# Reordering the first loads of a gated attention/MLP kernel: x tiles 0 and 1 from one ring, the other ring held back, a key matmul between the transposes

## The chip, the cores and the metric

The kernel runs on one core of one Trainium2 chip. The metric is the device time of one execution in microseconds (us). A trace's own span is about 1.7 us shorter than the time reported for that execution. All moments inside a trace are counted from the start of its span. The engines are PE (TensorE, the matmuls), ACT (ScalarE), DVE (VectorE), POOL (GpSimd) and SP (SyncE, which here only issues DMAs). A load "lands" when the trace reports it as complete. "The clock" is that of PE; its record in the trace says when it was full.

## The reference

```python
def reference(A_x, A_wqkv, A_wo, B_x, B_w1, B_b1, B_w2, B_b2, gate_w):
    x = A_x                                              # [1, 2048, 512] bf16
    g = sigmoid((x * gate_w).sum(-1, keepdims=True))
    a = linear_attention(x, A_wqkv, A_wo)                # 32 heads of 16; phi(k) = elu-like + 1e-6
    b = token_mlp(layernorm(x), B_w1, B_b1, B_w2, B_b2)  # 2048 -> 1792 -> 2048 along the tokens
    return g * a + (1 - g) * b
```

Only the first step matters here. The key matmuls read x transposed (`kacc<-wk_sb,xT` in the profile), so the kernel transposes the first four x tiles of 128 rows on TensorE and gets the other twelve from transposing DMAs.

## The kernel before

SP and ACT each issue plain DMAs on their own ring. The first eight loads of 128 KB are x tiles 0 to 3 and the four 128-row chunks of Wk. Behind them SP issues the DMA transposes and everything else. In the listing, `load_x(q, t0, n)` loads x tiles, `load_wk(q, k)` chunk k of Wk, `load_xT(t0, n)` is a DMA transpose from SP.

```python
load_x(nc.sync, 0, 1)
load_x(nc.scalar, 1, 1)
load_wk(nc.sync, 0)
load_x(nc.scalar, 2, 1)
load_x(nc.sync, 3, 1)
for k, q in ((1, nc.scalar), (2, nc.sync), (3, nc.scalar)):
    load_wk(q, k)
load_xT(4, 2)
load_xT(6, 2)
load_x(nc.sync, 4, 4)
# ... [cut: the remaining x tiles, Wq, w1, Wv, Wo, all from SP]
nc.vector.memset(ones_f[:], 1.0)
nc.vector.memset(mhalf[:], -0.5)
nc.vector.memset(Z32[:], 0.0)
# ... [cut: identity and masks on GpSimd]
warm_up(6)                      # six matmuls of 512 columns on a constant, result unused
# ... [cut: definitions]
HEADS = 4
transpose_tile(0, False)        # 4 PE transposes into one tile (pt), then a copy on DVE
transpose_tile(1, True)         # the same, copy on ACT
transpose_tile(2, False)
ln_step(0)
for k in range(2):
    for t in range(HEADS - 1):
        k_part(t, (k,))         # key matmul: tile t, chunk k of Wk, accumulating in kacc
transpose_tile(HEADS - 1, True)
ln_step(1)
for t in range(HEADS):
    k_part(t, range(2 if t < HEADS - 1 else 0, ND))
    k_phi(t)
for t in range(HEADS, NT):      # steady state
    k_part(t, range(ND))
    k_phi(t)
    g_tile(t - LAG)             # gacc: first one at t = 4
    # ... [cut]
```

In the profile `wps` is written by the warm-up matmuls, `pt` by the transposes, `kacc` by the key matmuls, and `gacc` by the matmuls that sum x times phi(k) over the tokens. Before the first gacc matmul PE thus has to do 16 transposes of 128 columns and 20 key matmuls of 512 columns: 6 in the first group (tiles 0 to 2 with Wk chunks 0 and 1) and 14 after tile 3's transposes (tiles 0 to 2 with chunks 2 and 3, tiles 3 and 4 with all four).

Of the kernel before, what the change touches and what calls it, by code (L numbers as in the profile page):

```python
# [15 lines left out]
def kernel(  # L16
# [13 lines left out]
    nc = tc.nc  # L30
# [36 lines left out]
    def keep(shape, dtype, name):  # L67
        return persist.tile(shape, dtype, name=name, tag=name)

    def bank(name, dtype=FP32):  # L70
        return ps.tile([P, SC], dtype, name=name, tag="bank")
# [5 lines left out]
    wk_sb = keep([P, ND, D], BF16, "wk_sb")  # L77
# [7 lines left out]
    Z32 = keep([P, ND * 40], BF16, "Z32")  # L85
# [22 lines left out]
    mhalf = keep([P, TPC], FP32, "mhalf")  # L108
    ones_f = keep([P, 1], FP32, "ones_f")
    warm = nc.const_aps.tensor(1.0, (P, SC), BF16)  # L110

    def mm(o, lhsT, rhs, start, stop, **kw):
        nc.tensor.matmul(o, lhsT=lhsT, rhs=rhs, start=start, stop=stop, **kw)  # L113
# [14 lines left out]
    def load_x(q, t0, n):  # L128
        q.dma_start(out=xs[:, t0 : t0 + n, :], in_=x_view[:, t0 : t0 + n, :])

    def load_wk(q, k):
        q.dma_start(out=wk_sb[:, k, :], in_=wqkv_view[:, k, D : 2 * D])

    def load_xT(t0, n):
        nc.sync.dma_start(
            out=xT[:, :, t0 * P : (t0 + n) * P], in_=X[t0 * P : (t0 + n) * P, :], transpose=True
        )

    load_x(nc.sync, 0, 1)
    load_x(nc.scalar, 1, 1)  # L140
    load_wk(nc.sync, 0)
    load_x(nc.scalar, 2, 1)
    load_x(nc.sync, 3, 1)
    for k, q in ((1, nc.scalar), (2, nc.sync), (3, nc.scalar)):
# [18 lines left out]
            nc.sync.dma_start(out=wv_sb[:], in_=wqkv_view[:, :, 2 * D : 3 * D])  # L163
            nc.sync.dma_start(out=wo_sb[:], in_=wo_view)

    nc.vector.memset(ones_f[:], 1.0)
    nc.vector.memset(mhalf[:], -0.5)
    nc.vector.memset(Z32[:], 0.0)
    nc.gpsimd.memset(ident[:], 0.0)
    nc.gpsimd.affine_select(  # L170
        out=ident[:], in_=ident[:], compare_op=ALU.not_equal, fill=1.0, base=0,
# [18 lines left out]
    def warm_up(n, cols=SC):  # L190
        for _ in range(n):
            mm(wps[:, :cols], warm[:, 0:P], warm[:, :cols], True, True)

    act_warm = keep([P, 1], FP32, "act_warm")
    nc.scalar.activation(out=act_warm[:], in_=ones_f[:], func=ACT.Exp)
    warm_up(6)

    def transpose_tile(t, on_act):
        pt = bank("pt", BF16)
        for k in range(ND):  # L200
            nc.tensor.transpose(pt[:, k * P : (k + 1) * P], xs[:, t, k * P : (k + 1) * P], ident[:])  # L201
        dst = xT[:, :, t * P : (t + 1) * P]
        src = pt[:].rearrange("p (k s) -> p k s", k=ND)
        if on_act:
            nc.scalar.activation(out=dst, in_=src, func=ACT.Copy)
        else:
            nc.vector.tensor_copy(out=dst, in_=src)
# [13 lines left out]
    def k_part(t, ks):  # L221
        if t not in kaccs:
            kaccs[t] = bank("kacc")
        for k in ks:
            mm(
                kaccs[t][:], xT[:, k, t * P : (t + 1) * P], wk_sb[:, k, :],
                k == 0, k == ND - 1,
            )
# [49 lines left out]
    def ln_step(u):  # L278
        ln_stats(u)
        if u % TPC == TPC - 1:  # L280
            ln_rstd(u // TPC)

    HEADS = 4
    transpose_tile(0, False)
    transpose_tile(1, True)
    transpose_tile(2, False)
    ln_step(0)
    for k in range(2):
        for t in range(HEADS - 1):
            k_part(t, (k,))  # L290
    transpose_tile(HEADS - 1, True)
    ln_step(1)
    for t in range(HEADS):
# [243 lines left out]
```

## Time and profile before

| | before |
|---|---|
| time, 4 runs | median 164.31 us (163.93 to 164.63) |
| span of the trace | 162.6 us |
| PE busy | 158.0 us, 97% |
| first transpose | 3.74 us |
| full clock of PE from | 5.73 us |
| first gacc matmul | 9.91 us |

From the profile's page of the kernel before, the busy time of each engine and the chain of waits by engine and line:

```profile
PE 158.0 (97%) x823; PEld 72.9 (45%) x837; DVE 89.5 (55%) x210; ACT 63.3 (39%) x97; POOL 17.5 (11%) x34
...
PE 96%; DMA 2%; issue 1%; DVE 0%
```

PE is the bound; beside short stretches of issuing, the only other thing on the chain of any size is one DMA. The timeline of PE alone in the kernel before, 0 to 9.5 us, merged by group (start, time, engine, line, operation, out<-in, form, count, idle before):

```profile
0.84 2.72 PE L113 MATMUL wps<-const-bfloat16-1.0 128*128 128x512 bf16 x6 [0.84 <-PEq L521]
3.74 1.46 PE L201 MATMUL pt<-ident,xs 128*128 128x128 bf16 x12 [0.17 <-DMA xs<-in_A_x_dram]
4.99 1.84 PE L113 MATMUL kacc<-wk_sb,xT 128*128 128x512 bf16 x6
6.66 0.39 PE L201 MATMUL pt<-ident,xs 128*128 128x128 bf16 x4
6.89 2.97 PE L113 MATMUL kacc<-wk_sb,xT 128*128 128x512 bf16 x13
```

From 3.74 us on PE has nearly always something to do (its longest gap before 9.9 us is 0.04 us). Its speed is not constant. The records of single instructions have transposes 0.107 us apart and 512-column matmuls 0.427 us apart until 5.7 us, and then 0.056 and 0.216 us. Full clock is thus about twice the early one, which is called half clock below. The clock record agrees: full from 5.73 us.

The issues of the two DMA rings in the kernel before up to 3.6 us, SP's and then ACT's, from the timelines of these two engines ("SPq" and "ACTq" are their sequencers; the time is that of issuing, not of moving):

```profile
0.81 0.40 SPq L129 DMA_DIRECT2D xs<-in_A_x_dram  x1
1.27 0.42 SPq L132 DMA_DIRECT2D wk_sb<-in_A_wqkv_dram  x1
1.74 0.43 SPq L129 DMA_DIRECT2D xs<-in_A_x_dram  x1
2.21 0.44 SPq L132 DMA_DIRECT2D wk_sb<-in_A_wqkv_dram  x1
3.52 2.96 SPq L135 DMA_TRANSPOSE xT<-in_A_x_dram  x2
```

```profile
0.80 0.87 ACTq L129 DMA_DIRECT2D xs<-in_A_x_dram  x2
1.70 0.94 ACTq L132 DMA_DIRECT2D wk_sb<-in_A_wqkv_dram  x2
```

### The profile page before, as it was taken

What the parts mean: (1) busy time and instruction counts of PE and PEld (TensorE: products, weight loads), DVE (VectorE), ACT (ScalarE), POOL (GpSimd) and SP (SyncE); (2) the same over time, 40 slices, a digit from 0 to 9 for tenths busy, and PEclk for the clock granted to TensorE, in tenths of its full rate; (3) what the DMA queues carried; (4) which work ended last, traced back from release to release, by engine and by line L of the source; (5) the groups of instructions that cost most, each with busy time, mean ns of one, the idle gap of its engine ahead of it and who ended that gap; (6) DMA issues with size and microseconds to landing.
All of it is one profiled execution on the core that took longest, in us unless ns stands there. A gap on an engine that the chain in (4) does not pass through costs nothing.

```text
span 162.6 us, 2183 instructions
## 1 busy us (share of the span) xinstructions
PE 158.0 (97%) x823; PEld 72.9 (45%) x837; DVE 89.5 (55%) x210; ACT 63.3 (39%) x97; POOL 17.5 (11%) x34
## 2 busy tenths in 40 slices
PE   7999999999999999999999999999999999999992
PEld 2544444444444444444444444444444444444452
DVE  0599999967999999519995401166211111111112
ACT  3463386648667483212865113111122222111110
POOL 3000711200110000001415500050000000000000
PEclk9999999999999999999999999999999999999999
DMA  4999999999900006600892699732000001110001
GB/s 141 252 247 246 278 312 355 382 386 386 281 5 0 0 0 223 228 4 0 272 324 77 209 328 323 279 106 94 32 32 32 32 32 43 48 42 33 32 32 32
DMA packets 30057, 25.05 MB, mean 154 GB/s; under 512 B 7968, under 2 KB 29472, under 8 KB 30048
## 3 DMA queue, kind: packets, MB, share of 16 engines
q1 hardware_dynamic: 28032, 22.02, 42.9%
q0 software_dynamic: 1440, 2.38, 5.5%
q10 hardware_dynamic: 576, 0.52, 1.1%
q8 instruction: 6, 0.10, 0.2%
q14 instruction: 3, 0.02, 0.1%
HBM read 21.11 MB, written 2.23 MB: 144 GB/s over the span
## 4 chain that ended last, share of the span: by engine, by line
PE 96%; DMA 2%; issue 1%; DVE 0%
PE uacc L113 30%; PE yps L113 30%; PE kacc L113 9%; PE aps L113 8%; PE gacc L113 8%; PE qacc L113 8%; DMA xs<-in_A_x_dram 2%; PE pt L201 1%; PE denps L113 1%; PE kvps L113 0%; PE w2ps L113 0%; DVE ot L500 0%; PE pt L330 0%
## 5 line engine op out<-in xcount | busy, mean ns | idle before, releaser
L113 PE MATMUL uacc<-hs,w1c 128*128 128x512 bf16 x219 | 51.0, 379 | 0.4
L113 PE MATMUL yps<-uT,w2c 128*128 128x512 bf16 (+2 forms) x234 | 50.6, 366 | 0.2
L500 DVE SCALAR_TENSOR_TENSOR ot<-yps,c,a_sc 128x512 bf16<-128x512 f32 (+2 forms) x17 | 12.2, 719 | 44.8 <-PE yps L113 41.5
L113 PEld LDWEIGHTS <-w2c 128*128 128x128 bf16 x238 | 22.8, 98 | 25.9
L113 PEld LDWEIGHTS <-w1c 128*128 128x128 bf16 x224 | 21.8, 98 | 26.3 <-issue 0.2
L487 ACT ACTIVATE a_sc<-aps,c,gg 128x512 f32<-128x512 f32 x16 | 12.4, 777 | 46.7 <-PE aps L113 43.0
L324 ACT ACTIVATE uT<-uacc,bcol 128x512 bf16<-128x512 f32 x14 | 9.3, 688 | 21.7 <-PE uacc L113 21.7
L113 PE MATMUL aps<-W2sb,pqT 128*128 128x512 bf16 x63 | 16.2, 379 | 0.1
L113 PE MATMUL qacc<-xT,wq_sb 128*128 128x512 bf16 x63 | 16.2, 379 | 0.0
L113 PE MATMUL kacc<-wk_sb,xT 128*128 128x512 bf16 x63 | 16.1, 385 | 0.0
L113 PE MATMUL gacc<-pk,xs 128*128 128x512 bf16 x62 | 15.5, 379 | 0.1
L251 ACT ACTIVATE hs<-xs,nmr,rstd 128x512 bf16<-128x512 bf16 x16 | 12.8, 805 | 1.9 <-DVE nmr L245 1.9
L211 ACT ACTIVATE e<-qacc 128x512 bf16<-128x512 f32 x16 | 9.6, 597 | 9.2 <-PE qacc L113 8.3
L211 ACT ACTIVATE e<-kacc 128x512 bf16<-128x512 f32 x16 | 9.3, 595 | 6.9 <-PE kacc L113 5.6
L439 POOL DMA_DIRECT2D rex<-rd_dram x16 | 9.4, 598 | 22.9 <-DVE pqT L441 20.1
L215 DVE SCALAR_TENSOR_TENSOR pqT<-qacc,e 128x512 bf16<-128x512 f32 x16 | 11.1, 692 | 0.6
L215 DVE SCALAR_TENSOR_TENSOR pk<-kacc,e 128x512 bf16<-128x512 f32 x16 | 11.1, 692 | 0.6
L235 DVE BATCH_NORM_STATS2 stats<-xs 128x6 f32<-128x512 bf16 x16 | 10.9, 682 | 0.0
L212 DVE TENSOR_SCALAR e<-e 128x512 bf16<-128x512 bf16 x32 | 9.0, 282 | 3.2 <-ACT e L211 3.2
L426 DVE CUSTOM_DVE_ANT_0 junk<-xs,gw_b 128x512 bf16<-128x512 bf16 x16 | 9.8, 684 | 0.0
L276 DVE TENSOR_TENSOR zacc<-zacc,pk 128x512 f32<-128x512 f32 x14 | 9.6, 685 | 0.2
L113 PEld LDWEIGHTS <-pqT 128*128 128x128 bf16 x64 | 6.3, 98 | 7.6
(61 smaller groups left out, 71.7 us busy)
## 6 DMA issues: line engine op xcount, KB each, us to landing
w2c<-in_B_w_dram SPq DMA_DIRECT2D x8, 896.0 KB, 6.1
w1c<-in_B_w_dram SPq DMA_DIRECT2D x2, 2048.0 KB, 14.7
w1c<-in_B_w_dram SPq DMA_DIRECT2D x3, 1024.0 KB, 11.9
rex<-rd_dram POOLq DMA_DIRECT2D x16, 128.0 KB, 4.0
out_dram<-ot SPq DMA_DIRECT2D x15, 128.0 KB, 1.7
xs<-in_A_x_dram SPq DMA_DIRECT2D x3, 512.0 KB, 4.4
wq_sb<-in_A_wqkv_dram SPq DMA_DIRECT2D x1, 512.0 KB, 6.3
wv_sb<-in_A_wqkv_dram SPq DMA_DIRECT2D x1, 512.0 KB, 11.8
```

What stands on the lines that cost most here:

```text
L113: nc.tensor.matmul(o, lhsT=lhsT, rhs=rhs, start=start, stop=stop, **kw)
L211: nc.scalar.activation(out=e[:], in_=acc[:], func=ACT.Exp)
L212: nc.vector.tensor_scalar(out=e[:], in0=e[:], scalar1=1.0, scalar2=PHI_EPS, op0=ALU.min, op1=ALU.add)
L215: nc.vector.scalar_tensor_tensor(out=dst, in0=acc[:], scalar=0.0, in1=e[:], op0=ALU.max, op1=ALU.add)
L235: nc.vector.bn_stats(out=stats[:], in_=xs[:, t, :])
L251: nc.scalar.activation(out=hs[:, t, :], in_=xs[:, t, :], func=ACT.Identity, scale=rstd[:, t : t + 1], bias=nmr[:, t : t + 1],)
L276: nc.vector.tensor_tensor(out=zacc[:], in0=first, in1=pk[:, t, :], op=ALU.add)
L324: nc.scalar.activation(out=uT[:, j, :], in_=acc[:], func=ACT.Gelu_apprx_tanh, bias=bcol[:, j : j + 1])
L426: nc.vector.tensor_tensor_reduce(out=junk[:], in0=xs[:, t, :], in1=gw_b[:], scale=1.0, scalar=0.0, op0=ALU.mult, op1=ALU.add, accum_out=gp ...
L439: nc.gpsimd.dma_start(out=rex[:], in_=src.unsqueeze(1).to_broadcast([8, HEAD, SC]))
L487: nc.scalar.activation(out=a_sc[:], in_=aps[:], func=ACT.Identity, scale=gg[:, t : t + 1], bias=c2[:, t : t + 1],)
L500: nc.vector.scalar_tensor_tensor(out=ot[:, :W], in0=yps[:, :W], scalar=c1[:, t : t + 1], in1=a_sc[:, cs], op0=ALU.mult, op1=ALU.add,)
```

## The change

Its intent: let x tile 0 have the DMA engines to itself for a moment so that the first transpose starts earlier, drop one warm-up matmul to match, and put a key matmul between the transposes of tiles 1 and 2. To make ACT's ring wait, its first load is given a destination that DVE writes first: the scheduler then makes the load wait for the write (in the traces ACT's first load is issued at 0.80 us before and at 1.12 us after, 0.02 us behind the end of the write).

```diff
+    nc.vector.memset(ones_f[:], 1.0)
+    nc.vector.memset(mhalf[:], -0.5)
+    nc.vector.memset(Z32[:], 0.0)
+    nc.vector.memset(wk_sb[:, 0, 0:2], 0.0)
     load_x(nc.sync, 0, 1)
-    load_x(nc.scalar, 1, 1)
-    load_wk(nc.sync, 0)
+    load_wk(nc.scalar, 0)
+    load_x(nc.sync, 1, 1)
     load_x(nc.scalar, 2, 1)
     load_x(nc.sync, 3, 1)
 ... [cut: the three memsets are taken away further down]
-    warm_up(6)
+    warm_up(5)
 ... [cut]
     transpose_tile(0, False)
     transpose_tile(1, True)
+    k_part(0, (0,))
     transpose_tile(2, False)
     ln_step(0)
-    for k in range(2):
-        for t in range(HEADS - 1):
-            k_part(t, (k,))
+    for t, k in ((1, 0), (0, 1), (1, 1), (2, 0), (2, 1)):
+        k_part(t, (k,))
```

The diff does not show one consequence, which the semaphores do. Each load reports its landing on one; the first eight DMAs that the two rings issue use eight, and the ninth takes one of them again. Before, the ninth is SP's first DMA transpose: it has the semaphore of x tile 1 and is issued at 3.52 us, 0.02 us after that tile landed. With the hold, the scheduler gives the eighth semaphore to SP's first DMA transpose, which then waits for nothing, and lets ACT's last Wk chunk wait for the landing of x tile 0, whose semaphore it takes over.

More of the change, by code (lines that the diff above doesn't have):

```diff
@@ L164 @@
             nc.sync.dma_start(out=wo_sb[:], in_=wo_view)
-    nc.vector.memset(ones_f[:], 1.0)
-    nc.vector.memset(mhalf[:], -0.5)
-    nc.vector.memset(Z32[:], 0.0)
     nc.gpsimd.memset(ident[:], 0.0)
```

## The prediction

> **What bounds the kernel now.** TensorE. The page's busy table gives PE 158.0 of 162.6 us (97%), and the chain of waits is 96% PE. What is left sits at the start: the chain shows 0.81 to 3.69 us as a wait for the first x tile, then PE work without a break. The timeline of PE has six warm-up matmuls from 0.84 us (pitch 0.427 us), the first transpose at 3.74, twelve transposes 0.107 us apart, the first key matmul at 4.99, the pitch falling to 0.216 us at about 5.7 (the clock record says full clock from 5.73). From 6.9 us PE runs at full rate and waits for nothing. So only the time until about 7 us can change.
>
> **What the change does.**
> 1. x tile 0 no longer shares the DMA engines with x tile 1. Before, tile 1 (ACT's ring) lands at 3.50 us, tile 0 (SP's) at 3.69, while up to 380 GB/s move. Alone, 128 KB need 0.35 us less at that rate (estimate). I expect tile 0 at about 3.2 us: 0.5 us earlier. The DVE write that holds ACT back ends near 1.2 us (the three memsets before it end at 1.07), so ACT begins 0.4 us later than before. [...]
> 2. One warm-up matmul less (0.43 us) fits the earlier landing.
> 3. Eight transposes, then key matmul (0,0). That needs tile 0's copy: before, the copy began 0.65 us after the first transpose and its reader started 1.15 us after it. Eight cold transposes take 0.85 us, so PE now idles about 0.3 us, which tile 2's transposes used to fill.
> 4. The last chunk of Wk moves from ACT's fourth issue at 2.18 us to behind the landing of x tile 0 (a reused DMA semaphore), to about 3.3 us, and SP's first DMA transpose moves up from 3.52 to about 2.7 us and competes. Before, chunk 2 landed at 6.83 us for a matmul at 6.89, chunk 3 at 6.57 for one at 7.10: hardly any slack. An earlier PE would meet them as waits of 0.1 to 0.4 us.
>
> **What is worth anything.** Until about 5.7 us PE is at half clock, so 0.5 us gained there is worth half of that, 0.25 us, unless the clock comes up earlier too. [...] Gain 0.5 us in x, minus the 0.3 us hole, minus half clock, minus Wk waits: net 0.1 to 0.5 us of 164.4. After 7 us all should only shift.
>
> **Predicted:** 164.1 us, 163.3 to 164.8 in 8 of 10. Faster by over 2%: 0.01; within 2%: 0.98; slower by over 2%: 0.01.
>
> **What would show the steps right or wrong.** First transpose at 3.1 to 3.4 us in the timeline (before 3.74); an idle of about 0.3 us on PE before the first key matmul with the DVE copy as releaser; small waits of key matmuls for the Wk loads between 5.5 and 7 us; the first gacc matmul at 9.4 to 9.9 us (before 9.91); from there to the end the same length within 0.2 us.
>
> **What would make it wrong.** [...] chunk 3 landing after 7.3 us; or tile 0 landing as early as 2.9 us with the clock rising earlier, which would give near 1 us.

0.5 us gained in x, less the hole of 0.3 us, the halving and the waits for Wk, came to a net 0.1 to 0.5 us of 164.4, so 164.1 us.

## The result, and the profile after

| | before | after |
|---|---|---|
| time, 4 runs each | 164.31 us (163.93 to 164.63) | 166.48 us (166.33 to 166.75) |
| first transpose | 3.74 us | 2.93 us |
| x tile 2 landed | 4.13 us | 5.51 us |
| PE at full clock from | 5.73 us | 10.10 us (from the spacing of matmuls; this trace has no clock record) |
| first gacc matmul | 9.91 us | 12.35 us |

The ratio is 1.0135, with a 95% interval of 1.0108 to 1.0162. A ratio here is the mean time of one kernel's fast runs over that of the other's of the same rounds, so not quite the ratio of the medians quoted. The changed kernel is 2.2 us slower, where 0.2 us faster had been forecast.

From the profile's page of the changed kernel, the same two lines:

```profile
PE 160.4 (97%) x836; PEld 73.2 (44%) x836; DVE 89.5 (54%) x211; ACT 63.5 (38%) x97; POOL 17.5 (11%) x34
...
PE 95%; DMA 2%; DVE 0%; ACTq 0%; issue 0%
```

PE is busy 2.4 us more, with one warm-up matmul less to do: the shares at the top of a page do not show that anything is wrong. The timeline of PE does (changed kernel, 0 to 9.5 us, same columns):

```profile
0.84 2.29 PE L113 MATMUL wps<-const-bfloat16-1.0 128*128 128x512 bf16 x5 [0.84 <-PEq L522]
2.93 0.63 PE L202 MATMUL pt<-ident,xs 128*128 128x128 bf16 x4
3.80 0.61 PE L202 MATMUL pt<-ident,xs 128*128 128x128 bf16 x4 [0.24 <-DMA xs<-in_A_x_dram]
4.20 0.63 PE L113 MATMUL kacc<-wk_sb,xT 128*128 128x512 bf16 x1
5.55 0.61 PE L202 MATMUL pt<-ident,xs 128*128 128x128 bf16 x4 [0.72 <-DMA xs<-in_A_x_dram]
5.95 2.40 PE L113 MATMUL kacc<-wk_sb,xT 128*128 128x512 bf16 x5
8.14 0.63 PE L202 MATMUL pt<-ident,xs 128*128 128x128 bf16 x4
8.57 1.48 PE L113 MATMUL kacc<-wk_sb,xT 128*128 128x512 bf16 x3
```

Two things are new. PE waits for x tile 1 and, longer, for x tile 2 (the line at 5.55). And five key matmuls from 5.95 us take 2.40 us, where six took 1.84 before: PE still runs at half clock. How long one key matmul lasts shows this directly. The view of tile kacc between 6.0 and 9.5 us, kernel before and then changed kernel (duration in ns, min/median/max):

```profile
L113 PE MATMUL kacc<-wk_sb,xT x17: 379/379/380, 5.8 to 9.5; 128*128 128x512 bf16 x17
```

```profile
L113 PE MATMUL kacc<-wk_sb,xT x8: 586/631/634, 6.0 to 9.4; 128*128 128x512 bf16 x8
```

The chain of waits of the changed kernel begins with DVE's writes, of which the last is the hold (the first line here), goes through ACT's ring to the load of x tile 2, and then stays on PE:

```profile
1.08 0.02 DVE wk_sb L142
1.10 0.02 issue
1.12 0.43 ACTq L132
1.55 0.03 issue
1.57 3.93 DMA xs<-in_A_x_dram
5.51 0.04 issue
5.55 0.61 PE pt L202 x4
```

And the rings, SP's and ACT's, in the changed kernel, the same first loads:

```profile
0.81 1.35 SPq L129 DMA_DIRECT2D xs<-in_A_x_dram  x3
2.20 0.43 SPq L132 DMA_DIRECT2D wk_sb<-in_A_wqkv_dram  x1
2.68 3.95 SPq L135 DMA_TRANSPOSE xT<-in_A_x_dram  x2
```

```profile
1.12 0.43 ACTq L132 DMA_DIRECT2D wk_sb<-in_A_wqkv_dram  x1
1.57 0.46 ACTq L129 DMA_DIRECT2D xs<-in_A_x_dram  x1
2.06 1.19 ACTq L132 DMA_DIRECT2D wk_sb<-in_A_wqkv_dram  x2
```

x tile 2 is issued 0.35 us later than before (1.57 against 1.22 us) and lands 1.38 us later. The first DMA transpose is issued at 2.68 us instead of 3.52.

### A sum that fits the traces

At half clock both kinds of instruction take about twice as long (0.107 against 0.056 us, 0.427 against 0.216 us), and the work before the first gacc matmul is 16 transposes and 20 key matmuls: 16 x 0.1067 + 20 x 0.4267 = 10.24 us at half clock (the spacings of the traces with one digit more). If PE idles only while it is at half clock, the first gacc matmul starts at

half of (moment of full clock + first transpose + idle of PE between these two + 10.24).

Idle is counted here from start to start: what lies between the starts of two neighbours beyond the spacing of the first. The timeline's own figures in brackets are about 0.2 us smaller, as they count a matmul to its modelled end.

| trace | full clock | first transpose | idle | sum says | trace says |
|---|---|---|---|---|---|
| before | 5.73 | 3.74 | 0.04 | 9.88 | 9.91 |
| after | 10.10 | 2.93 | 1.47 | 12.37 | 12.35 |
| after, second trace (`after_again`) | 9.39 | 2.93 | 1.45 | 12.01 | 11.99 |
| `before_hold` | 9.09 | 3.36 | 1.39 | 12.04 | 12.06 |
| `before_w3` | 6.68 | 3.81 | 0.05 | 10.39 | 10.42 |
| `pe_only` | 8.43 | 3.56 | 0.30 | 11.27 | 11.28 |

Everything behind it only shifts: from the first gacc matmul to the end of the span are 152.7 us in both traces. So in this pair of traces the later full clock costs half of 4.37, 2.19 us; PE's new idle costs half of 1.43, 0.72 us; the earlier first transpose gains half of 0.81, 0.40 us. Together 2.5 us, where the spans differ by 2.4. In the terms of the sum, half clock behind the first transpose cost half of (5.73 - 3.74 - 0.04), 0.98 us or 0.6% of the span, before, and half of (10.10 - 2.93 - 1.47), 2.85 us or 1.7%, after.

### The profile page after: what moved, and what is told of

Read it like the earlier page. It is cut to its first block, busy times and chain, and to the rows that moved or that the text cites. A ratio compares the mean times of both kernels' runs of the same rounds, so it can differ in the third digit from the quotient of the medians.

```text
span 165.0 us, 2195 instructions
## 1 busy us (share of the span) xinstructions
PE 160.4 (97%) x836; PEld 73.2 (44%) x836; DVE 89.5 (54%) x211; ACT 63.5 (38%) x97; POOL 17.5 (11%) x34
## 4 chain that ended last, share of the span: by engine, by line
PE 95%; DMA 2%; DVE 0%; ACTq 0%; issue 0%
PE uacc L113 29%; PE yps L113 29%; PE kacc L113 9%; PE aps L113 8%; PE qacc L113 8%; PE gacc L113 8%; DMA xs<-in_A_x_dram 2%; PE pt L202 1%; PE denps L113 1%; PE kvps L113 0%; ACTq L132 0%; PE w2ps L113 0%; DVE ot L501 0%; DVE Z L141 0%; DVE ones_f L139 0%
## 5 line engine op out<-in xcount | busy, mean ns | idle before, releaser
L113 PE MATMUL kacc<-wk_sb,xT 128*128 128x512 bf16 x64 | 18.3, 416 | 0.0
L113 PEld LDWEIGHTS <-xT 128*128 128x128 bf16 x64 | 6.7, 106 | 8.1 <-issue 1.7
```

The costliest lines, as they stand in the source:

```text
L113: nc.tensor.matmul(o, lhsT=lhsT, rhs=rhs, start=start, stop=stop, **kw)
```

## The experiments

Two causes are possible and they overlap in time, so each had to be taken alone. Theory A: PE's idle keeps its clock low for longer. Rival B: the later landings cost the time themselves, at any clock. Where the landings are late, there is a second question: is it the DMA transpose that moved forward (theory T), or the hold of ACT's ring (rival H)? Most runs were timed in 3 or 5 rounds beside the kernel before on the same chip, plus the profiled execution. The times quoted as "all runs" include it. The kernel before itself ran 34 times in all. One run took 283.03 us and is not used. Another, in the rounds beside the first eight experiments, took 166.34 us; it has no trace, so its cause is not known, and it widens the intervals of those ratios. The other 32 took 163.88 to 164.94 us.

### after_fill: fill PE's idle in the changed kernel

```diff
     transpose_tile(0, False)
+    warm_up(1)
     transpose_tile(1, True)
     k_part(0, (0,))
+    warm_up(2)
     transpose_tile(2, False)
```

> The changed kernel with three more matmuls on constants, one between the transposes of x tiles 0 and 1 and two between key matmul (0,0) and the transposes of tile 2, where PE idled 0.44 and 0.92 us. The loads are untouched. Theory A (the idle of PE keeps its clock at half for about 4.2 us longer, and that is the 2.2 us): the pitch of matmuls falls to 0.216 us at about 5.7 us instead of 9.9, and the time is 163.9 to 164.7 us, about that of the kernel before. Rival B (the later landings themselves cost 2 us, PE would wait for them at any clock): 166.2 to 166.8 us as before, the filling only takes the place of idle.

Measured: 166.58 (profiled), 166.26, 165.22, 164.69 us; correct. The clock was full at 5.79 us in the trace, as A says, but the profiled run was no faster. Of the runs without a trace one lies in B's range, one in A's and one between. The chain of waits of this run names the reason:

```profile
2.96 6.37 DMA wk_sb<-in_A_wqkv_dram
9.32 0.04 issue
9.37 2.97 PE kacc L113 x13
```

The last Wk chunk, issued at 2.96 us, landed at 9.32, and PE stood waiting for it. So neither theory alone holds: with the clock mended, the loads can cost as much in one run.

### before_w3: idle on PE, with the loads of before

```diff
-    warm_up(6)
+    warm_up(3)
```

> The kernel before with three warm-up matmuls instead of six and nothing else changed: the loads land as they did, PE idles from about 2.1 to 3.7 us. Theory A: the idle of 1.6 us delays the full clock from 5.7 us to 7.5 to 10 us, and the time rises by 0.9 to 2.2 us, to 165.2 to 166.6. Rival B: warm-up matmuls compute nothing and the loads are the same, so 164.2 to 164.6 us.

Measured: 164.83 (profiled), 165.96, 165.72, 166.11, 166.21 us; the kernel before in these rounds 164.45 us (median). Ratio 1.0074 (1.0002 to 1.0146). The loads land as before (all of Wk by 6.74 us, before by 6.83); only unused matmuls are gone. PE's timeline, its first two lines:

```profile
0.84 1.44 PE L113 MATMUL wps<-const-bfloat16-1.0 128*128 128x512 bf16 x3 [0.84 <-PEq L521]
3.81 1.46 PE L201 MATMUL pt<-ident,xs 128*128 128x128 bf16 x12 [1.53 <-DMA xs<-in_A_x_dram]
```

This is what A says and B does not: idle of PE alone costs 1.3 to 1.8 us in four of the five runs. In the one run that has a trace, the fastest, the clock was full at 6.68 us, which is 0.96 us later than in the kernel before but earlier than forecast; that the clock came later still in the others is inferred from their times.

### loads_only: only the new loads, PE order and warm-ups of before

> The loads of the changed kernel (first two x tiles from SP, ACT held by the DVE write and begun with the Wk chunk) with the PE order and the six warm-ups of before. Theory A with the late x tile 2 (5.5 us) as the cause of the idle: PE has no work between the transposes of tile 1 and those of tile 2, idles about 1.2 us, the clock is late, 166.0 to 166.8 us. If the new PE order or the missing warm-up were the cause: 163.9 to 164.5 us.

```diff
-    warm_up(5)
+    warm_up(6)
 ... [cut]
-    k_part(0, (0,))
     transpose_tile(2, False)
     ln_step(0)
-    for t, k in ((1, 0), (0, 1), (1, 1), (2, 0), (2, 1)):
-        k_part(t, (k,))
+    for k in range(2):
+        for t in range(HEADS - 1):
+            k_part(t, (k,))
```

The edit is on the changed kernel. Measured: 166.85 (profiled), 165.31, 165.77, 165.84 us. In the trace x tile 2 lands at 5.75 us, PE idles 1.44 us before its transposes, the clock is full at 9.66 us. By the medians the loads alone bring 1.4 us of the slowdown (165.81 against 164.45; three of the four runs lie below the 166.0 of the forecast, the traced one does not); the new PE order is not needed for that.

### pe_only: only the new PE order and five warm-ups, loads of before

> The loads of before with the PE order of the changed kernel and five warm-ups. If the late load of x tile 2 is the cause, this one has PE idle of about 0.8 us before the first transpose and 0.3 us before the first key matmul only, and the clock rises at about 5.7 us: 164.3 to 164.8 us. If the PE order or the missing warm-up is the cause: 165.5 to 166.7 us.

The edit, on the kernel before, is that of the change without its loads:

```diff
-    warm_up(6)
+    warm_up(5)
 ... [cut]
+    k_part(0, (0,))
     transpose_tile(2, False)
     ln_step(0)
-    for k in range(2):
-        for t in range(HEADS - 1):
-            k_part(t, (k,))
+    for t, k in ((1, 0), (0, 1), (1, 1), (2, 0), (2, 1)):
+        k_part(t, (k,))
```

Measured: 165.68 (profiled), 164.77, 164.76, 164.88 us against 164.45. So 0.3 us in the ordinary case; in the profiled run the clock came at 8.43 us, which fits the sum above and is the likely reason for the extra 0.9 us of that run. The order and the missing warm-up are a small part by these four runs.

### after_latexp: the DMA transposes held back

The transposing DMAs and all that SP issues behind them are moved behind the copy of tile 0, with a DVE write to wait for.

```diff
     transpose_tile(0, False)
+    nc.vector.memset(xT[:, 0, HEADS * P : HEADS * P + 2], 0.0)
+    later_loads()      # load_xT(4, 2) and everything that followed it on SP, unchanged
```

> The changed kernel, but SP's first DMA transpose held back by a DVE write into its destination that follows the copy of tile 0, so it is issued at about 4.1 us instead of 2.68 us, behind all eight first loads; Wk's last chunk is then issued at about 2.5 us instead of 2.90. Theory T (the DMA transpose, issued 0.84 us earlier than in the kernel before, is what holds up the loads of x tile 2 and of the Wk chunks): x tile 2 lands by 4.5 us (changed: 5.0 to 5.75), all Wk chunks by 6.6 us, time 163.4 to 164.4 us. Rival H (ACT's ring being held back and begun with Wk is what makes x tile 2 late): x tile 2 still lands after 5.2 us, time 165.3 to 166.7 us.

Measured: 165.05 (profiled), 165.02, 166.82, 165.13 us. x tile 2 landed at 4.56 us and the last Wk chunk at 6.78. This looked like T, but the time fits neither forecast: the clock was full at 3.86 us in the trace, yet PE waited for Wk chunks, and the first gacc matmul started at 10.15 us.

### after_nohold: no DVE write into Wk

```diff
-    nc.vector.memset(wk_sb[:, 0, 0:2], 0.0)
```

> The changed kernel without the DVE write into Wk: ACT begins at 0.80 us instead of 1.12, and (by the reuse of semaphores) SP's first DMA transpose waits for x tile 0 again, at about 3.1 to 3.5 us, and Wk's last chunk waits for nothing. Rival H: x tile 2 lands near 4.1 us, time 163.8 to 164.5 us. Theory T says the same, as the transposes move too, only if they come after 3.2 us; the landing of x tile 0 should go back to about 3.3 to 3.6 us, which costs up to 0.3 us.

Measured: 164.63 (profiled), 164.46, 166.33, 166.43 us, in two groups. x tile 2 landed at 4.19 us, the last Wk chunk at 6.75 (chunk 2 at 6.95), x tile 0 at 3.61. The traced run had the clock full at 4.30 us. With the loads mended, two runs of four equal the kernel before, and two are about 2 us slower. For those a late clock is the likely cause, as PE has idle of 0.72 us before the first transpose; it is inferred.

### after_wk3sp: the last Wk chunk from SP, ahead of the transposes

```diff
-    for k, q in ((1, nc.scalar), (2, nc.sync), (3, nc.scalar)):
+    for k, q in ((1, nc.scalar), (2, nc.sync), (3, nc.sync)):
```

> The changed kernel with the last Wk chunk issued by SP in front of the DMA transposes, so the hold of ACT stays, and the first transpose is issued at about 3.1 us (behind x tile 0, which lands at 2.9). Theory T: between the two kernels, x tile 2 at 4.3 to 5 us, Wk chunks by 6.7 us, PE waits less, 164.0 to 165.2 us. Rival H: x tile 2 after 5.2 us, 165.3 to 166.7 us.

Measured: 166.85 (profiled), 166.88, 165.74, 164.60 us: too wide to decide by time. x tile 2 landed at 4.69 us and all of Wk by 6.74, as T had it; the clock was full only at 9.44 us.

### before_earlyxp: one DMA transpose early, in the kernel before

```diff
     load_x(nc.sync, 3, 1)
+    load_xT(4, 2)
     for k, q in ((1, nc.scalar), (2, nc.sync), (3, nc.scalar)):
         load_wk(q, k)
-    load_xT(4, 2)
     load_xT(6, 2)
```

> The kernel before with one DMA transpose moved ahead of the third Wk chunk on SP's ring: issued at about 2.2 us instead of 3.52; that chunk is then issued at about 3.6 us. Everything else as before, ACT not held back. Theory T: the loads issued near 2 us land 0.5 us or more later than before (x tile 3 after 6.3, Wk chunks 1 to 3 after 6.8, one after 7.5 us), PE waits, the time is 165.0 to 167 us. Rival H: only the third Wk chunk is late, and PE waits for it alone, 0.3 us at most: 164.2 to 164.9 us.

Measured: 165.48 (profiled), 165.54, 164.69, 165.46 us against 164.38. x tile 2 landed at 4.16 us, untouched, x tile 3 at 6.45 (before 6.05), the Wk chunk behind the transpose at 8.02 (before 6.83), and PE waited 1.05 us for it. So here a transpose in front of a load delayed that load, but not x tile 2. Half of T's forecast missed: the two Wk chunks on ACT landed at 6.05 and 6.66, hardly later than before.

### before_w9: nine warm-ups in the kernel before

```diff
-    warm_up(6)
+    warm_up(9)
```

> The kernel before with nine warm-up matmuls instead of six, so PE is busy from 0.84 us on without a gap and the first transpose starts at about 4.7 us, 0.95 us later than in the kernel before. Loads unchanged. Theory A+L (two floors: PE's clock, and the landing of the last Wk chunk at about 6.8 us plus 14 warm matmuls, 3.0 us): the clock is full by 5.0 us or so in every run, the first gacc matmul starts at 9.8 to 10.1 us (before 9.91), the time is 164.2 to 164.6 us in all runs, with none above 165. Rival (an earlier or later first transpose counts): about 164.8 to 165.4 us.

Measured: 164.72 (profiled), 165.15, 165.17, 165.33, 164.71, 165.04 us; ratio 1.0029 (1.0016 to 1.0042). The clock was full at 4.34 us, no run was slow, but the forecast missed by 0.5 us: the first gacc matmul started at 10.30 us, because a fast PE ran out of work: it stood 0.24 us before the first key matmul (tile 0's copy), then 0.17 us for tile 1's copy and 0.19 us for Wk chunk 1, which landed at 6.37 us; the later first transpose cost the rest. In this trace a clock earlier than 5.7 us bought nothing.

### after_w9: nine warm-ups in the changed kernel

```diff
-    warm_up(5)
+    warm_up(9)
```

It is meant to measure the loads alone.

> The changed kernel with nine warm-up matmuls: the clock is full before the first key matmul, the loads are those of the changed kernel. It measures what the loads cost alone. Theory A+L: the clock record is before 5.5 us, PE waits 0.5 to 2.5 us in all for x tile 2 and the Wk chunks, which land as late as before the filling (x tile 2 after 5.0, the last chunk at 6.9 to 9.4 us); 164.9 to 166.6 us, wide from run to run. If the clock alone were the cause: 164.0 to 164.6 us.

Measured: 165.41 (profiled), 165.97, 165.15, 165.98, 166.34, 165.22 us, as forecast; ratio 1.0069 (1.0047 to 1.0092). The clock was full at 5.98 us, not before 5.5 as forecast; x tile 2 landed at 5.14 and the last Wk chunk at 8.17 us. Next to `before_w9` on the same chip this is the nearest figure for the cost of the changed loads with no late clock: 165.69 against 165.09 us by the medians, 0.6 us. It is not the loads alone, as the new PE order is in it too, and the clock of the two traces differs (5.98 and 4.34 us).

### latexp_fill: both causes mended, or so it was meant

```diff
     later_loads()
+    warm_up(1)
     transpose_tile(1, True)
     ...
-    for t, k in ((1, 0), (0, 1), (1, 1), (2, 0), (2, 1)):
+    k_part(1, (0,))
+    warm_up(1)
+    for t, k in ((0, 1), (1, 1), (2, 0), (2, 1)):
         k_part(t, (k,))
```

> The changed kernel with the DMA transposes held back (as in the run with them at 4.17 us) and two filling matmuls, one between the transposes of tiles 0 and 1 and one before key matmul (0,1), where PE waited. Both causes mended: clock full at 6 us or before, the last Wk chunk at about 6.8 us, first gacc matmul at 9.7 to 10.1 us, 164.0 to 164.6 us. If something third costs time: 165 us or more.

Measured: 165.42 (profiled), 165.32, 165.10, 165.11, 165.11 us; ratio 1.0041. The clock was full at 3.53 us and the last Wk chunk landed at 6.79, but the chain has x tile 2 landing at 5.71 us:

```profile
1.57 4.14 DMA xs<-in_A_x_dram
5.71 0.05 issue
5.76 0.40 PE pt L204 x4
```

The DMA transposes were not issued before 4.10 us here. Theory T, as the only reason for the late x tile 2, falls. A share of it is not excluded: in the four traces with ACT held and the DMA transposes behind 3.1 us x tile 2 landed at 4.56, 4.69, 5.40 and 5.71 us, in the six with the first transpose at 2.68 us at 5.02 to 5.75.

### after_again: the changed kernel once more

No edit.

> The changed kernel unedited, for its spread on this chip and a second trace. If PE's idle makes the late clock sure: all runs 166.2 to 166.8 us. If the moment of the clock drifts from run to run: 164.8 to 166.8 us, and the trace's moment of full clock differs from 10.1 us.

Measured: 166.40 (profiled), 164.81, 166.46, 166.54, 166.46, 165.02 us. In the trace the clock was full at 9.39 us, not 10.10 as in the first. So the moment drifts between executions of one kernel, and two of these six runs were 1.5 us faster than the other four.

### before_hold: the hold alone

```diff
+    nc.vector.memset(ones_f[:], 1.0)
+    nc.vector.memset(mhalf[:], -0.5)
+    nc.vector.memset(Z32[:], 0.0)
+    nc.vector.memset(xs[:, 1, 0:2], 0.0)
     load_x(nc.sync, 0, 1)
     load_x(nc.scalar, 1, 1)
 ... [cut: the three memsets are taken away further down]
```

> The kernel before with only the hold: a DVE write into x tile 1 keeps ACT's first load back from 0.80 to about 1.12 us. By the reuse of semaphores the first DMA transpose comes at about 2.7 us and the last Wk chunk on ACT at 2.9 us, as in the changed kernel; PE order and the six warm-ups are those of before. If the hold with its consequences is the whole cause: x tile 2 after 4.5 us, last Wk chunk after 6.9 us, 165.2 to 166.7 us. If the cause lies in Wk coming first on ACT or in the PE order: 164.2 to 164.7 us.

Measured: 166.46 (profiled), 165.02, 166.25, 166.81, 166.76, 166.13 us against 164.59; ratio 1.0107 (1.0075 to 1.0140). One DVE write of two columns, with nothing else of the change but its side effects, costs 1.77 us by the medians, about as much as the changed kernel next to its own rounds of the kernel before in `after_again` (166.43 against 164.60, 1.83 us). PE's timeline, its first four lines:

```profile
0.85 2.72 PE L113 MATMUL wps<-const-bfloat16-1.0 128*128 128x512 bf16 x6 [0.85 <-PEq L522]
3.36 1.06 PE L202 MATMUL pt<-ident,xs 128*128 128x128 bf16 x8
5.60 0.61 PE L202 MATMUL pt<-ident,xs 128*128 128x128 bf16 x4 [1.18 <-DMA xs<-in_A_x_dram]
6.00 2.77 PE L113 MATMUL kacc<-wk_sb,xT 128*128 128x512 bf16 x6
```

The first transpose is 0.38 us earlier than in the kernel before, PE then stands for 1.4 us until x tile 2 is there, and the clock is full at 9.09 us.

### before_hold_late: the hold, without the early transposes

```diff
+    nc.vector.memset(xs[:, 1, 0:2], 0.0)      # with the three memsets, as in before_hold
     load_x(nc.sync, 0, 1)
 ... [cut]
     transpose_tile(0, False)
+    nc.vector.memset(xT[:, 0, HEADS * P : HEADS * P + 2], 0.0)
+    later_loads()                              # as in after_latexp
```

> The same with the DMA transposes held back to about 4.2 us by a DVE write, and the last Wk chunk free to go at 2.5 us. Rival H (the hold itself): x tile 2 after 4.5 us still, 165 to 166.5 us. Theory T (the transposes in front): x tile 2 by 4.4 us, all Wk by 6.8 us, 164.0 to 164.7 us.

Measured: 167.37 (profiled, over 1.5% above this kernel's fastest), 165.31, 164.47, 165.02, 164.79, 164.86, 165.61 us against 164.59; ratio 1.0025 (1.0002 to 1.0049). In the traced run x tile 2 landed at 5.40 us with the transposes issued at 4.50: it is late without the early transposes. The last Wk chunk, free of the wait and of the transposes, landed at 6.87 us instead of 8.06. Without the early transposes and the late Wk chunk six of the seven runs are at most 1.02 us above the kernel before, where five of six of `before_hold` were 1.5 us or more. Whether x tile 2 landed earlier in these six, as it did in two of the held traces above, or Wk alone made the difference, cannot be said, as the one trace fell on an exceptional run (clock full at 10.07 us).

### nohold_w6: the changed kernel without the hold, with six warm-ups

```diff
-    nc.vector.memset(wk_sb[:, 0, 0:2], 0.0)
 ... [cut]
-    warm_up(5)
+    warm_up(6)
```

> The changed kernel without the hold and with six warm-ups. Loads land as in the kernel before (x tile 2 near 4.2, last Wk chunk near 6.9 us); PE has gaps of 0.3 us before the transposes and another 0.3 to 0.5 us near tile 1 and key matmul (0,0). Most runs 164.4 to 164.9 us; a late clock (166.3) in at most one of three, as against two of four with five warm-ups.

Measured: 164.75 (profiled), 164.76, 164.53, 164.86, 164.28, 164.64 us; ratio 1.0010 (0.9990 to 1.0030). With the hold gone and the warm-up back, all of the slowdown is gone, in every run, though the new PE order stays. Both edits count: without the hold but with five warm-ups (`after_nohold`) two of four runs were still slow. No gain is left either: in the trace the clock was full at 4.63 us, and PE waited for Wk:

```profile
1.74 4.46 DMA wk_sb<-in_A_wqkv_dram
6.20 0.04 issue
6.24 1.02 PE kacc L113 x4
```

### before_w7: a candidate for a better kernel

```diff
-    warm_up(6)
+    warm_up(7)
```

> The kernel before with seven warm-up matmuls: the 0.38 us gap before the first transpose is filled, the transpose starts about 0.1 us later. Clock at 5.7 us or before in all runs, 164.2 to 164.6 us: no measurable gain on the median, perhaps no run at 166.

Measured: 164.80 (profiled), 164.28, 164.61, 164.23, 164.73, 164.45 us against 164.59; ratio 1.0002 (0.9982 to 1.0023). The same time, and no run near 166. But in the trace the clock was full at 6.63 us although PE had been busy since 0.84 without a gap of over 0.04 us; why it came so late was not shown. Nothing that was run beats the kernel before.

### The landings of all traces together

| | traces | x tile 2 landed |
|---|---|---|
| ACT's ring begins at 0.80 us | 8 | 4.13 to 4.32 us |
| ACT's ring held to 1.12 us | 10 | 4.56 to 5.75 us, seven of them after 5.1 |

| last Wk chunk on ACT | traces | landed |
|---|---|---|
| waits for x tile 0, transposes issued ahead of it | 6 | 6.91 to 9.32 us |
| free to be issued by 2.6 us | 11 | 6.53 to 7.10 us |

(The eighteenth trace has that chunk on SP, at 6.74 us.) With the hold x tile 2 is late in every trace. The reused semaphore and the transposes in front make the last Wk chunk late in four of the six traces, by 1 to 2 us; in the two traces of the changed kernel itself it landed at 6.91 and 6.92 us, no later than elsewhere. In the kernel before four loads land by 4.32 us and the next one only at 5.85. The landing of a load is reported in 16 steps (the profile's page counts 16 DMA engines): in all traces they lie within 0.63 us for the loads that have landed by 4.5 us, and 1.2 us or more apart for some of the loads that follow. Of the 16 steps of the Wk chunk that landed at 5.85 us in the kernel before, seven came by 4.75 us and nine from 5.42 to 5.85. In the kernel before this stretch falls on a Wk chunk and x tile 3, which PE does not need yet; with the hold it falls on x tile 2, for which PE is waiting. Why the stretch is slow was not found.

## Why the prediction was wrong

- **Bound (right).** PE, and only the first 7 us to be changed. The part behind the first gacc matmul kept its length (152.7 us in both traces).
- **x tile 0 earlier (right in kind, too small).** Forecast 3.2 us, landed at 2.88; first transpose 0.81 us earlier. Under half clock this is worth 0.40 us, as the prediction's rule has it.
- **Step 1, "ACT begins 0.4 us later", then dropped (the first step that failed).** It was read off about rightly (0.32 us), but its effect was carried to no x tile except tile 0. x tile 2 is ACT's second load; it landed at 5.51 us instead of 4.13, and PE waited 0.93 us for it. The prediction's own sentence about the chunks of Wk that have "hardly any slack" should have been written for every load: tile 2 landed at 4.13 us before for a transpose at about 4.6.
- **Step 3, the hole of 0.3 us before key matmul (0,0) (wrong place).** In the changed kernel that matmul did not wait at all, because x tile 1 was late enough. The idle came before tile 1 (0.44 us) and before tile 2 (0.93 us).
- **Step 4, waits for Wk of 0.1 to 0.4 us (right in this trace, too narrow).** At half clock PE waited 0.1 us. With the clock in time the same loads make it wait up to 1.0 us for one chunk (`after_fill`).
- **"What is worth anything": the clock (the term that was mis-sized).** The sum used 5.7 us for the full clock; a later one because of gaps on PE was named only as a tail case. It came at 10.1 and 9.4 us in the two traces, worth 2.2 and 1.8 us, and in 8 of the 10 runs of the changed kernel the time was 166.3 or more. In this kernel, with about 1.45 us of idle before the clock is up, the late clock is the ordinary case (two traces show it; for the other six slow runs it is inferred). `before_w3` shows by its times that idle alone does it, `before_hold` that the hold brings this idle, `nohold_w6` that without the hold and with the warm-up the loss is gone.
- **Range (too narrow).** 163.3 to 164.8 assumed that gaps on PE were unlikely to move the clock.

What stays open is how the loss of `before_hold` divides between clock and loads in runs without a trace, as the two overlap, why the stretch after 4.3 us is slow, and what decides the moment at which the clock rises. In the eighteen traces it rose between 3.53 and 10.10 us, and the amount of idle does not sort them:

| trace | idle of PE between its first matmul and the rise | full clock from |
|---|---|---|
| `before_w9` | no gap of over 0.04 us | 4.34 us |
| `before_w7` | no gap of over 0.04 us | 6.63 us |
| before | 0.38 us before the first transpose, 0.04 behind it | 5.73 us |
| `pe_only` | 0.63 us before the first transpose, 0.30 behind it | 8.43 us |
| `before_w3` | 1.73 us before the first transpose, 0.05 behind it | 6.68 us |
| after | none before the first transpose, 1.47 us behind it | 10.10 us (from the spacing) |

Nor is the moment fixed for one kernel: the two traces of the changed kernel have 10.10 and 9.39 us. What the times show is how often a kernel is slow. Of the 33 fast runs of the kernel before, with 0.42 us of idle in its trace, one took 166.34 us and the others at most 164.94; `before_w3`, with the same loads and 1.78 us, took 165.7 us or more in four of five runs; the changed kernel, with 1.47 us and later loads, 166.3 or more in 8 of 10. So the kernels with 1.47 and 1.78 us of idle were slow in most of their runs, not in all.

## What to carry to other kernels

In these runs idle of PE before its full clock cost in two ways: half of the idle itself by the sum above (0.72 us for 1.43 us), and more runs in which the full clock came late, or is inferred to have come late (the two groups of times lie 1.5 us apart in `after_again` and 1.8 in `after_nohold`); so when a change moves the first loads, check the landing of every operand in PE's order, not only of the first. The hold on one ring moved the loads behind it (x tile 2 issued 0.35 us later) and changed which DMA waits on which reused semaphore (the last Wk chunk on ACT, issued at 2.90 instead of 2.18 us), so look at the built order of waits. And before hunting for tenths in a prologue, look for the next floor: here even a PE that was fast at 4.3 us (`before_w9`, `after_nohold`) stood waiting for a Wk chunk that landed at 6.1 to 6.4 us.
